# One batch's attention scores in 32 bits from TensorE transposes, in an attention and expert-layer kernel with a new instruction order

## The chip, the cores and the metric

The kernel runs on 1 core of one Trainium2 chip, as one program. The metric is the device time of one execution in microseconds (us). The engines are called PE (TensorE, matrix products), PEld (its weight loads), DVE (VectorE), ACT (ScalarE), POOL (GpSimd) and SP (SyncE, which here issues all DMAs).

## What is computed

Attention with 8 batches, 8 heads, 512 local and 32 global tokens per batch and 64 values per head. Global queries see all 544 keys; a local query sees the 32 global keys and the local keys within 32 positions. The result, 4352 tokens of 512 values, goes through a two-layer network with a piecewise-quadratic activation. All inputs and outputs are float32; the harness holds w_in and w_out as 64-bit words, which the kernel decodes itself.

```python
s_g = scale * (q_g @ k_all.T);  out_g = sm(s_g) @ v_all
s_ll = where(|pos_q - pos_k| <= 32, scale * (q_l @ k_l.T), -1e9)
s_l = concat([scale * (q_l @ k_g.T), s_ll]);  out_l = sm(s_l) @ concat([v_g, v_l])
x = concat([out_g, out_l]).transpose(0, 2, 1, 3).reshape(B * S, H * D)      # 4352 x 512
h = x @ w_in                                                                # 512 x 2048
g = where(h >= 1, h, where(h <= -1, 0, (h + 1) ** 2 / 4))
out = g @ w_out                                                             # 2048 x 512
```

## The kernel before, in words

**Precision.** Nearly all products run in float16: each operand is scaled by a power of two and split into a high and a low half, and two or three half products are summed. For queries and keys this means per batch: norms (`scale_k`, `scale_q`, lines 652 and 674), scaled splits (`nat_split`, line 707: ACT or POOL makes the high half, DVE or POOL the low half), transposes of the two halves to head-major tiles (`turn`, line 426: eight TensorE transposes into a bank and one copy out, or a DMA transpose), and for the queries a second tile with the halves swapped (`swap_q`, line 786: two SBUF-to-SBUF DMAs). `att_a` (line 858) then multiplies, for a block of 128 local queries (index i, 0 to 3) and a pair of heads (index pr, 0 to 3), the query tile and its swapped twin with each key range; there are two ranges of 128 and 64 columns for i = 0 and 3, and three of 128, 64 and 32 for i = 1 and 2. A fused DVE operation adds the mask and finds the maximum, ACT exponentiates, the probabilities are split and transposed, `att_b` (line 931) multiplies them with the values, `att_x` (line 956) divides. `glob_a` (line 1008) makes the scores of the global queries, four heads side by side in column strips of the array.

**Batch 0.** Its probabilities for i = 0 and 1 are already kept in float32 (`T["exactpv"]=2`): transposed in 32 bits on TensorE and multiplied with unsplit values. There the second product of a head has 64 rows for i = 0 and 96 rows for i = 1. A second switch, `T["exact"]`, selects 32-bit score products for the first batches; it is 0, so no batch takes that path.

**Experts.** A step s covers 256 tokens; batch b gives steps 2b and 2b+1. `win_decode` and `wout_decode` (lines 445 and 498) turn 32 blocks of 64-bit words into float32 on DVE, with ACT or POOL making parts; `win_halves` and `wout_split` make float16 halves. `moe1` (line 1138) is the first layer, four groups of 512 hidden units each for two tiles of 128 tokens; `act` the activation; `moe2` (line 1239) the second layer. From step 2 on `moe_f` does the first layer with seven instead of eight block products.

**Order.** The steps are recorded in a list by due times (`at`, line 1280), cut into segments of one engine each, and replayed in the order of a table of segment numbers (`ORDER`, line 1473); a second table (`SLOTS`) says which of 48 SBUF rooms, 6 larger ones and 8 PSUM banks each tile takes, and strings in `T` say which engine does each copy, split and cast. So one engine's instructions stand in one fixed sequence, and a waiting instruction holds back all behind it. Input loads are issued by SP with at most five on the way:

```python
if len(loads) >= AHEAD:
    tc.add_manual_dep(r.ins, loads[-AHEAD].ins.name, ...)
```

All instructions are issued from line 1461 of the file (DMA loads from 1463), so rows are told apart by the names of their tiles: `room`, `bank` and `twin` are the SBUF rooms and PSUM banks, `weights_w` the expert weights.

## Time and profile before

| | |
|---|---|
| median of 3 runs | 907.37 us (904.98 to 909.11) |
| profiled execution | 907.72 us, of it the span 906.0 us |
| mean granted TensorE clock | 0.996 of full speed |
| PE busy | 867.5 us (96%) |
| DVE busy | 750.1 us (83%) |
| ACT busy | 661.7 us (73%) |
| POOL busy | 358.3 us (40%) |
| DMA | 133.9 MB, mean 148 GB/s |

The span runs from the first to the last instruction; 1.7 us of the execution lie around it. PE is the busiest engine. The shares are means over a program whose first hundred microseconds are unlike the rest.

### The profile page before, as it was taken

Reading aid. Unit: us, or ns where it says so; the run is one execution under the profiler, and the core shown is the slowest. Engines: PE = TensorE matmul, PEld = TensorE weight load, DVE = VectorE, ACT = ScalarE, POOL = GpSimd, SP = SyncE. Lnnn points to the kernel's source line nnn. Section 1 sums busy time; section 2 is a strip of 40 time slices with the busy share of each in tenths; the row PEclk is TensorE's granted clock in tenths of the full one; section 3 lists DMA queues with packets and bytes.
Section 4 is the critical chain, followed back from the end, with each engine's and each line's share of the span. In section 5 each row is a group of like instructions: output and inputs, shape, how many; then the busy total and the mean of one; then the engine's idle time right before and its main releaser. Section 6 shows DMA issues by size and latency. Waiting matters only on the chain. (4 is left out here: it accounts for less than half of the span.)

```text
span 906.0 us, 30503 instructions
## 1 busy us (share of the span) xinstructions
PE 867.5 (96%) x12132; PEld 652.0 (72%) x12132; DVE 750.1 (83%) x2128; ACT 661.7 (73%) x1628; POOL 358.3 (40%) x406
## 2 busy tenths in 40 slices
PE   3798999999999999999999999999999999999998
PEld 2467876779686778767786866868786768687853
DVE  4989999989989897979878987887879788877651
ACT  4778998878887797688677668787868766555440
POOL 5314786444514333432343134262425432415230
PEclk9989999999999999999999999999999999999999
DMA  9989987999998999798977867968994965472101
GB/s 265 269 214 242 215 153 141 182 155 164 185 160 136 171 183 187 131 155 164 161 148 120 135 143 128 162 140 158 173 170 97 150 114 107 89 136 31 31 1 47
DMA packets 405680, 133.93 MB, mean 148 GB/s; under 512 B 382241, under 2 KB 391457, under 8 KB 405537
## 3 DMA queue, kind: packets, MB, share of 16 engines
q1 hardware_dynamic: 405536, 131.98, 79.2%
q8 instruction: 95, 1.56, 0.7%
q14 instruction: 49, 0.39, 0.2%
HBM read 44.56 MB, written 8.91 MB: 59 GB/s over the span
## 5 line engine op out<-in xcount | busy, mean ns | idle before, releaser
L1461 PEld LDWEIGHTS <-room 128*128 128x128 f16 (+2 forms) x4952 | 284.8, 98 | 203.2 <-issue 15.8
L1461 PE MATMUL bank<-weights_w,room 128*128 128x512 f16 x1632 | 370.1, 379 | 0.0
L1461 POOL TENSOR_TENSOR room<-room,room 128x512 f16<-128x512 f32 (+2 forms) x193 | 200.8, 1051 | 274.7 <-ACT room L1461 234.6
L1461 PEld LDWEIGHTS <-weights_w 128*128 128x128 f16 (+1 forms) x3968 | 221.3, 98 | 24.3 <-DVE weights_w L1461 12.9
L1461 PE MATMUL bank<-room,weights_w 128*128 128x128 f16 (+1 forms) x3840 | 225.3, 216 | 1.5 <-DVE small_nb L1461 0.8
L1461 ACT CAST room<-room 128x512 f16<-128x512 f32 (+1 forms) x213 | 121.5, 582 | 56.6 <-DVE room L1461 39.7
L1461 POOL TENSOR_TENSOR const_pb<-room,const_pb 128x448 f16<-128x448 f32 (+1 forms) x77 | 78.9, 1026 | 163.3 <-ACT const_pb L1461 78.7
L1461 PE MATMUL bank<-room,room 128*128 128x64 f16 (+6 forms) x2688 | 135.8, 200 | 4.6 <-DVE small_nb L1461 1.4
L1461 ACT ACTIVATE room<-room,small_nb 128x224 f32<-128x224 f32 (+1 forms) x256 | 118.0, 462 | 27.9 <-DVE small_nb L1461 27.1
L1461 PE MATMUL bank<-room,twin 128*128 128x128 f16 (+1 forms) x2304 | 132.1, 216 | 0.4 <-DVE room L1461 0.4
L1461 PEld LDWEIGHTS <-twin 128*128 128x128 f16 x2304 | 123.6, 98 | 2.3 <-issue 0.5
L1461 DVE CUSTOM_DVE_ANT_0 room<-bank,const_mask,batch_small_q 128x192 f32<-128x192 f32 (+1 forms) x256 | 99.6, 427 | 22.7 <-PE bank L1461 15.7
L1461 ACT ACTIVATE room<-bank,batch_small_ms 128x512 f32<-128x512 f32 (+1 forms) x112 | 83.6, 750 | 47.6 <-DVE bank L1461 20.5
L1461 DVE SCALAR_TENSOR_TENSOR bank<-bank,batch_small_ms,room 128x512 f32<-128x512 f32 (+1 forms) x112 | 80.7, 723 | 19.4 <-ACT room L1461 19.3
L1461 DVE SCALAR_TENSOR_TENSOR room<-room,batch_small_ms,bank 128x512 f32<-128x512 f32 (+1 forms) x112 | 79.3, 713 | 1.8
L1461 ACT ACTIVATE junk_junka<-room 128x512 f16<-128x512 f32 (+2 forms) x110 | 68.6, 623 | 13.0 <-DMA room<-in_q_l_dram 9.4
L1461 ACT COPY room<-bank 128x512 f32<-128x512 f32 (+3 forms) x118 | 64.5, 561 | 17.9 <-PE bank L1461 15.3
L1461 DVE TENSOR_TENSOR room<-room,room 128x512 f16<-128x512 f32 (+1 forms) x66 | 52.8, 803 | 12.9 <-ACT room L1461 12.7
L1461 DVE SCALAR_TENSOR_TENSOR room<-room,batch_small_ms,room 128x512 f32<-128x512 f32 (+1 forms) x64 | 50.4, 789 | 5.6 <-ACT room L1461 5.0
L1461 ACT CAST const_pb<-room 128x384 f16<-128x384 f32 (+1 forms) x80 | 42.2, 529 | 13.9 <-DMA room<-const_pb 13.3
L1461 DVE TENSOR_TENSOR bank<-bank,room 128x512 f32<-128x512 f32 (+1 forms) x64 | 41.8, 658 | 11.2 <-PE bank L1461 9.4
L1461 ACT ACTIVATION_READ_ACCUMULATOR room<-room,small_nb 128x1 f32 x256 | 48.4, 189 | 0.0
(179 smaller groups left out, 954.4 us busy)
## 6 DMA issues: line engine op xcount, KB each, us to landing
room<-room SPq DMA_DIRECT2D x80, 128.0 KB, 3.1
room<-in_q_l_dram SPq DMA_DIRECT2D x32, 256.0 KB, 4.1
weights_w<-in_moe_w_in_dram SPq DMA_DIRECT2D x32, 256.0 KB, 3.9
twin<-in_moe_w_out_dram SPq DMA_DIRECT2D x32, 256.0 KB, 4.6
out_dram<-room SPq DMA_DIRECT2D x32, 256.0 KB, 2.6
room<-in_k_l_dram SPq DMA_DIRECT2D x24, 256.0 KB, 4.0
room<-in_v_l_dram SPq DMA_DIRECT2D x24, 256.0 KB, 4.0
room<-const_pb SPq DMA_TRANSPOSE x119, 3.6
```

The source lines that it names most:

```text
L1461: getattr(getattr(tc.nc, engine), op)(*a, **k)
```

## The change

The first batch takes the 32-bit path (`exact=1`), and that path is rewritten. Queries and keys are loaded in the same blocks of 128 tokens as for the other batches. `heads` (which replaces `pairs`) transposes two heads at a time in 32 bits on TensorE, four transposes per block of tokens, 40 in all; one copy takes a block of keys out of the bank, two copies a block of queries (each to a tile whose other 64 rows POOL has set to zero, so that a product over 128 rows counts one head of the pair). `scale_k`, `scale_q`, `nat_split`, `turn` and `swap_q` are not run for batch 0. `att_a` makes one 32-bit product per head and key range, 80 in all, in place of 160 in float16; `glob_a` makes 40 in place of 80. The 32-bit products of probabilities with values now have 96 rows for i = 0 too: POOL sets 32 rows of the transposed tile to zero, and `att_b` takes 96 rows of both operands. `ORDER`, `SLOTS` and the engine strings of `T` are replaced as a whole, so every engine's sequence differs throughout the program.

```diff
-    def load_pairs(src_l, src_g, b, nm, part):
-    ...
     def load(b, nm, part):
-        if EXACT(b) and nm != "v":
-            r = load_pairs(*{"k": (k_l, k_g), "q": (q_l, q_g)}[nm], b, nm, part)
-            ...
         r = load_q(b, part) if nm == "q" else load_kv(...)
-    def pairs(b, nm, c):
+    def heads(b, nm, c):
         st, n = BT[b]["raw" + nm][c]
         one = full_id()
-        ...
+        t = ps_t.tile([P, NI, n], F32, tag="p", name=f"pt{nm}{b}_{c}")
+        for hp in range(NI):
+            nc.tensor.transpose(t[:, hp], st[:n, 2 * hp:2 * hp + 2, :].rearrange("p h d -> p (h d)"), one[:n, :n])
+        return t
     def prep_k(b, c):
         if EXACT(b):
+            t = heads(b, "k", c)
+            k = (ktp if c < NI else kt4p).tile(list(t.shape), F32, ...)
+            evict(of("turns", b, c, 30, "a"), k, t)
     def prep_q(b, c):
             for u, pl in enumerate((qap, qbp)):
+                q = pl.tile([P, NI, P], F32, tag="qa" if u == 0 else "qb", name=f"q{'ab'[u]}{b}_{c}")
                 nc.gpsimd.memset(q[(1 - u) * D:(2 - u) * D], 0.0)
+                evict(who if who != "d" else "av"[u], q[u * D:u * D + D], t[u * D:u * D + D])
     def att_a(b, i, pr):
+            h = pr if EXACT(b) else 2 * pr + u
             for lo, hi, kk in regs:
-                nc.tensor.matmul(s[:, u, lo:hi], qa, kk, start=True, stop=False)
-                nc.tensor.matmul(s[:, u, lo:hi], qb, kk, start=False, stop=True)
+                if EXACT(b):
+                    nc.tensor.matmul(s[:, u, lo:hi], d["q" + "ab"[u], i][:, h], kk, start=True, stop=True)
+                    continue
+                nc.tensor.matmul(s[:, u, lo:hi], d["qa", i][:, h], kk, start=True, stop=False)
+                nc.tensor.matmul(s[:, u, lo:hi], d["qb", i][:, h], kk, start=False, stop=True)
             one, n2 = full_id(), w - P
+            if n2 < CH2:
+                nc.gpsimd.memset(pt[n2:CH2, :, 1], 0.0)
     def att_b(b, i, pr):
             if EXACT_PV(b, i):
-                n2 = WID[i] - P
     def glob_a(b, g):
+                for j in range(4) if EXACT(b) else ():
+                    h = 4 * g + j
+                    nc.tensor.matmul(s[32 * j:32 * j + 32, o:o + n], d["qa", NI][:, h // 2, h % 2], d["kt", c][:, h // 2, 0:n],
+                                     start=True, stop=True, tile_position=(0, 32 * j))
+                for qn in () if EXACT(b) else ("qa", "qb"):
-ORDER = ("2 0 3 29 31 28 35 30 34 27 13 12 67 68 69 70 89 88 90 91 92 71 93 96 10 5 4 22 6 7 8 9 111 72 73 74 94 75 97 23 24 "
...
-T = dict(exact=0, exactpv=2, es="nnnn", gramq="aaaaaaaa", dg="vvvvvvaaaaavvav", sid="vvvvv", fast=2, grams="ppaaaaaa",
+T = dict(exact=1, exactpv=2, es="vnnn", gramq="aaaaaaaa", dg="vvvaavaavaaaaav", sid="vvvvv", fast=2, grams="ppaaaaaa",
...
```

DVE's sequence at the program's start, before (`small_amk` and `small_dg` belong to the key norm of batch 0, `batch_small_q` and `batch_small_sk` to its query and key scales, `weights_w_0_66` is the first block of w_in):

```order
L1461 TENSOR_REDUCE small_amk_104<-bank_105 128x1
L1461 TENSOR_SCALAR small_amk_104<-small_amk_104 128x1 x2
L1461 TENSOR_SCALAR batch_small_q_0_116<-batch_small_q_0_116 128x2 x3
L1461 TENSOR_SCALAR small_dg_106<-const_negid_84,small_amk_104 128x128
L1461 RECIPROCAL batch_small_q_0_116<-batch_small_q_0_116 128x2
L1461 TENSOR_REDUCE small_amk_104<-bank_107 128x1
L1461 TENSOR_SCALAR batch_small_sk_108<-small_amk_104 128x1
L1461 TENSOR_SCALAR batch_small_q_0_116<-batch_small_q_0_116,batch_small_sk_108 128x2
L1461 RECIPROCAL batch_small_sk_108<-batch_small_sk_108 128x1
L1461 SCALAR_TENSOR_TENSOR room_118<-room_86,batch_small_q_0_116,room_118 128x8x64
L1461 TENSOR_SCALAR weights_w_0_66<-weights_w_0_66 128x512
L1461 SCALAR_TENSOR_TENSOR bank_91<-bank_91,weights_w_0_66 128x512
```

and the same place in the change:

```order
L1424 MEMSET const_c_0_111 128x1 x2
L1424 COPY room_115<-bank_102 128x512
L1424 TENSOR_SCALAR weights_w_0_66<-weights_w_0_66 128x512
L1424 SCALAR_TENSOR_TENSOR bank_91<-bank_91,weights_w_0_66 128x512
L1424 TENSOR_SCALAR room_99<-weights_w_0_67 128x512
L1424 SCALAR_TENSOR_TENSOR weights_w_0_66<-weights_w_0_66,bank_91 128x512
L1424 ISA room_146,small_nb_145<-bank_132,const_mask_0_58,const_c_0_111 128x192
L1424 ISA small_nb_145 128x1
```

The norm and scale rows and the first query split are gone; one copy of a transposed block of keys stands ahead of the first decode, and the first score operations (ISA, the fused mask and maximum) stand right behind it.

SP's sequence at the start, before (loads of keys, then two blocks of queries, then the first w_in blocks):

```order
L1463 DMA room_94<-in_k_l_dram 128x8x64
L1463 DMA room_96<-in_k_l_dram 128x8x64
L1463 DMA room_93<-in_k_l_dram 96x8x64
L1463 DMA room_97<-in_k_g_dram 32x8x64
L1463 DMA room_95<-in_k_l_dram 128x8x64
L1463 DMA room_97<-in_k_l_dram 32x8x64
L1463 DMA room_93<-in_k_g_dram 32x8x64
L1463 DMA room_87<-in_q_l_dram 128x8x64
L1463 DMA room_86<-in_q_l_dram 128x8x64
L1463 DMA weights_w_0_69<-in_moe_w_in_dram 128x2x256
L1463 DMA weights_w_0_66<-in_moe_w_in_dram 128x2x256 x2
```

and in the change:

```order
L1426 DMA room_86<-in_q_l_dram 128x8x64
L1426 DMA weights_w_0_68<-in_moe_w_in_dram 128x2x256
L1426 DMA room_93<-in_k_g_dram 32x8x64
L1426 DMA room_94<-in_k_l_dram 128x8x64
L1426 DMA room_93<-in_k_l_dram 96x8x64
L1426 DMA weights_w_0_66<-in_moe_w_in_dram 128x2x256
L1426 DMA weights_w_0_70<-in_moe_w_in_dram 128x2x256
L1426 DMA weights_w_0_66<-in_moe_w_in_dram 128x2x256
```

The second half of the first w_in block, which the first decode needs, moves from the twelfth load to the eighth; three of the five key blocks move behind it.

TensorE's first score products of batch 0, before (`room_119` and `room_121` are the query tile and its swapped twin, `room_115` and `room_123` two key tiles; one head pair):

```order
L1461 MATMUL bank_105<-room_115,room_119 128x128
L1461 LDWEIGHTS room_121
L1461 MATMUL bank_105<-room_115,room_121 128x128
L1461 LDWEIGHTS room_119
L1461 MATMUL bank_105<-room_123,room_119 128x64
L1461 LDWEIGHTS room_121
L1461 MATMUL bank_105<-room_123,room_121 128x64
```

and in the change (`room_113` and `room_114` are the two query tiles, `room_112` and `room_115` the key tiles; one head pair):

```order
L1424 MATMUL bank_102<-room_110,room_94 128x128 x4
L1424 MATMUL bank_100<-room_110,room_93 128x128 x4
L1424 MATMUL bank_132<-room_112,room_113 128x128
L1424 MATMUL bank_132<-room_115,room_113 128x64
L1424 MATMUL bank_132<-room_112,room_114 128x128
L1424 MATMUL bank_132<-room_115,room_114 128x64
```

The 32-bit products need no separate weight-load instruction in the program, and the first of them stand directly behind the transposes of the first key blocks, ahead of the first w_in norms.

## Rows read from the trace of the kernel before

**Rows 1.** Busy time by stretch of the span: stretch in us, its length, then busy us and count for PE, PEld, DVE, ACT and POOL, the granted TensorE clock, the DMA share and GB/s.

```profile
0.00:14.50 14.50, 2.66 (x21) 2.07 (x21) 2.69 (x14) 3.96 (x7) 7.80 (x23) 1.00 1.01 218
14.50:80.00 65.50, 52.36 (x418) 37.76 (x419) 60.12 (x185) 53.67 (x125) 24.18 (x31) 0.95 0.99 255
80.00:112.60 32.60, 29.23 (x503) 27.59 (x501) 32.35 (x100) 29.61 (x66) 22.05 (x23) 1.00 1.10 223
112.60:800.00 687.40, 681.52 (x9893) 513.20 (x9891) 594.83 (x1719) 532.89 (x1351) 276.44 (x301) 1.00 0.85 149
800.00:906.00 106.00, 101.71 (x1309) 71.41 (x1306) 60.11 (x114) 41.56 (x81) 27.78 (x30) 1.00 0.23 44
```

**Rows 2.** What PE waited for from 0 to 112.6 us: total us, times, longest.

```profile
PE bank L1461 <- DVE weights_w L1461: 12.3, 7, 5.4
PE bank L1461 <- DMA room<-in_k_g_dram: 9.1, 1, 9.1
PE bank L1461 <- DVE room L1461: 2.8, 3, 1.6
PE bank L1461 <- DVE small_dg L1461: 1.4, 1, 1.4
```

**Rows 3.** Timeline of PE, merged, around the first product of the first expert layer and around the first of the second layer: start, us, what.

```profile
80.13 2.84 PE L1461 MATMUL bank<-room,weights_w 128*128 128x128 f16 x48
...
112.59 2.75 PE L1461 MATMUL bank<-weights_w,room 128*128 128x512 f16 x12
```

**Rows 4.** Timeline of DVE from 8 us on: start, us, what, and in brackets the idle time before it with what ended it.

```profile
11.49 0.29 DVE L1461 TENSOR_REDUCE small_amk<-bank 128x1 f32<-128x128 f32 x1 [10.43 <-PE bank L1461]
...
13.87 0.73 DVE L1461 SCALAR_TENSOR_TENSOR room<-room,batch_small_q,room 128x512 f16<-128x512 f32 x1
14.52 0.42 DVE L1461 TENSOR_SCALAR weights_w<-weights_w 128x512 int32<-128x512 int32 x1
15.05 0.70 DVE L1461 SCALAR_TENSOR_TENSOR bank<-bank,weights_w 128x512 int32<-128x512 int32 x1
```

**Rows 5.** Timeline of SP's DMA issues from 6 to 15 us: start, us, what. The two query loads are the eighth and ninth load, the weight loads begin with the tenth.

```profile
6.63 1.01 SPq L1463 DMA_DIRECT2D room<-in_q_l_dram  x2
8.38 6.93 SPq L1463 DMA_DIRECT2D weights_w<-in_moe_w_in_dram  x10
```

**Rows 6.** DMA issues from 8 to 16 us: what, count, size, median us from issue to landing.

```profile
weights_w<-in_moe_w_in_dram SPq DMA_DIRECT2D x11, 256.0 KB, 3.8
```

**Rows 7.** Groups of DVE instructions from 0 to 112.6 us, shapes apart: what, count, busy us, mean ns of one, idle before.

```profile
L1461 DVE SCALAR_TENSOR_TENSOR room<-room,batch_small_q,room 128x512 f16<-128x512 f32 x3 | 2.2, 740 | 0.0
L1461 DVE SCALAR_TENSOR_TENSOR room<-room,batch_small_sk,room 128x512 f16<-128x512 f32 x2 | 1.9, 936 | 0.3 <-ACT room L1461 0.3
L1461 DVE SCALAR_TENSOR_TENSOR room<-room,batch_small_sk,room 64x512 f16<-64x512 f32 x1 | 0.7, 735 | 0.0
L1461 DVE SCALAR_TENSOR_TENSOR room<-room,batch_small_q,room 32x512 f16<-32x512 f32 x1 | 0.7, 734 | 0.0
L1461 DVE TENSOR_SCALAR batch_small_q<-batch_small_q 128x3 f32<-128x3 f32 x3 | 0.6, 193 | 0.0
L1461 DVE TENSOR_SCALAR room<-room,batch_small_sk 128x512 f16<-128x512 f32 x1 | 0.5, 481 | 0.0
L1461 DVE TENSOR_SCALAR room<-room,batch_small_q 128x512 f16<-128x512 f32 x1 | 0.5, 478 | 0.0
L1461 DVE CAST weights_w<-bank 128x512 f16<-128x512 f32 x1 | 0.7, 660 | 0.0
```

**Rows 8.** Timeline of PE from 53.8 to 54.7 us and from 89 to 94.3 us, in 32 bits and in float16. A 32-bit product shows as two matmul records, a transpose as one.

```profile
53.94 0.61 PE L1461 MATMUL bank<-room,room 128*128 128x128 f32 x4
54.47 0.40 PE L1461 MATMUL bank<-const_ident,room 64*128 64x64 f16 x8
...
90.30 1.06 PE L1461 MATMUL bank<-room,room 128*128 128x64 f32 x8
91.19 2.85 PE L1461 MATMUL bank<-room,weights_w 128*128 128x128 f16 x48
93.88 0.28 PE L1461 MATMUL bank<-room,room 128*128 128x128 f16 x2
93.99 0.22 PE L1461 MATMUL bank<-kt_kt,room 128*128 128x64 f16 x2
94.05 0.28 PE L1461 MATMUL bank<-room,room 128*128 128x128 f16 x2
94.16 0.22 PE L1461 MATMUL bank<-kt_kt,room 128*128 128x64 f16 x2
94.22 0.28 PE L1461 MATMUL bank<-room,weights_w 128*128 128x128 f16 x2
```

**Rows 9.** Groups of PE instructions over the whole span, shapes apart, columns as in rows 7. The transposes through `const_ident` are those of batch 0; half of the bf16 products of `room` with itself are the key norm of batch 0; `qg_qga` are the global queries of all batches.

```profile
L1461 PE MATMUL bank<-room,qg_qga 128*32 128x128 f16 x256 | 9.2, 222 | 0.0
L1461 PE MATMUL bank<-const_ident,room 128*128 128x128 f16 x64 | 6.7, 274 | 2.3 <-DVE room L1461 2.3
L1461 PE MATMUL bank<-room,room 64*128 64x64 f32 x16 | 4.0, 333 | 0.0
L1461 PE MATMUL bank<-room,room 96*128 96x64 f32 x16 | 3.1, 275 | 0.0
L1461 PE MATMUL bank<-room 128*128 128x128 bf16 x32 | 2.9, 262 | 9.1 <-DMA room<-in_k_g_dram 9.1
```

**Rows 10.** Busy time by stretch from 55 to 72 us, columns as in rows 1.

```profile
55.00:60.00 5.00, 3.96 (x29) 2.36 (x27) 4.61 (x23) 3.00 (x9) 2.39 (x3) 1.00 0.84 217
60.00:61.00 1.00, 1.00 (x6) 0.81 (x5) 1.00 (x3) 1.00 (x3) 0.00 (x0) 0.66 0.83 205
61.00:66.00 5.00, 5.00 (x28) 3.34 (x29) 5.00 (x22) 2.49 (x6) 0.00 (x0) 0.50 0.54 149
66.00:67.00 1.00, 1.00 (x7) 0.98 (x5) 1.00 (x6) 1.00 (x2) 0.31 (x1) 0.50 0.42 92
67.00:72.00 5.00, 5.00 (x36) 3.49 (x35) 4.24 (x8) 4.52 (x15) 2.21 (x3) 0.99 0.91 234
```

**Rows 11.** Groups of POOL instructions from 0 to 14.5 us, columns as in rows 7.

```profile
L1461 POOL MEMSET const_pb<- 128x1024 f16 x2 | 1.8, 952 | 0.0
```

75 lines of the change are left out of this document (13 added, 62 removed), and 492 rows, old and new, of tables (ORDER, SLOTS).

## The prediction

> **What bounds the kernel now.** I read the busy time by stretch first. From 112.6 to 800 us PE works 681.5 of 687.4 us, and in the tail 101.7 of 106 [rows 1]: there PE is the bound, and time is won or lost only by PE's own work. The first 112.6 us are different. From 14.5 to 112.6 us (98.1 us) DVE works 60.12 + 32.35 = 92.5 us, PE 52.36 + 29.23 = 81.6, ACT 53.67 + 29.61 = 83.3 and POOL 46.2 [rows 1]: DVE is the fullest engine and PE has 16.5 us to spare. The waits of PE say the same: 12.3 us went to tiles of w_in that DVE was still decoding, 2.8 to other DVE results, 9.1 (one wait, at the start) to the load of the last keys [rows 2]. The timeline of PE gives the two milestones that count: the first expert product at 80.13 us and the first of the second layer at 112.59 [rows 3]. What moves the second one earlier moves the end earlier, provided PE does not get more to do behind it.
>
> The start, 0 to 14.5 us, is a chain of its own. DVE does nothing of weight until 11.49 us, when the key norm's sums arrive from PE; it then works through norm and scale rows and one query split, and only at 14.52 begins the first w_in decode [rows 4]. The loads agree: the query blocks are the eighth and ninth issue, at 6.63 us, the weights follow from 8.38 [rows 5], and a weight block lands 3.8 us after its issue [rows 6].
>
> So I cut the run into A (0 to 14.5), B (14.5 to 112.6, DVE's) and C (behind it, PE's). The profiled execution took 907.72 us with a span of 906.0; the median of the runs is 907.37, a third of a microsecond less, which I neglect. About 0.5% (4.5 us) is what a measurement of this kernel can tell from no change: faster means below 902.8, slower above 911.9.
>
> **A, the start.** Removed from DVE: the norm, scale and split rows between 11.49 and 14.52, 3.0 us in all [rows 4]. Added: one copy of a transposed key block, like the 128x512 cast out of a bank, 0.66 us [rows 7]. The second half of the first w_in block moves from the twelfth load to the eighth. The eighth was issued at 6.63 [rows 5]; with 3.8 us to land [rows 6] that is 10.4. The copy stands ahead of the decode on DVE and waits for load, transpose and bank, so I put the decode at 11.0: **-3.5 us**. Bounds: 0 (the three key blocks now behind the weights, or the copy's own wait, give it back) and -4.1 (decode right at landing). POOL gets more at this place: eight zeroings of 64 rows by 512 float32, 2 KB per partition, which is the size of the memset that took 0.952 us [rows 11], 7.6 us in all. POOL is busy 7.80 of 14.5 us in A and 24.18 of 65.5 behind it [rows 1], so they fit beside other work and I cost them at nothing. Without that cover, that is, if a mask that the first score operation needs queues behind them on POOL, they cost 4 (the half that the first two query blocks need) to 7.6 us.
>
> **B, DVE's work.** The splits of batch 0's keys and queries go: 2.2 + 1.9 + 0.7 + 0.7 + 0.5 + 0.5 = 6.5 us [rows 7], of which the one at 13.87 (0.73) was counted in A, so 5.8. Of some 20 small norm and scale operations, 0.19 us each [rows 7], about seven lie in B: 1.4. Together **-7.2**, say -7. The stretch holds 5.6 us of DVE idle time. Bounds: 0, if the casts and subtractions that the new engine strings hand to DVE (18 more in the whole program, at about 0.66 each 12 us; most lie behind B) fall in B, and -12.8, if the idle time goes with the work. ACT loses the high halves as well, so it is not the next bound; SP loses ten query-swap DMAs, and nothing waits for those any more.
>
> **B, PE's work.** One 32-bit product replaces two half products. In the timeline four 32-bit products of 64 columns go from 90.30 to 91.19, 0.222 us each; eight half products that make two heads' scores go from 93.88 to 94.22, 0.34 us; four 32-bit transposes of 128 columns go from 53.94 to 54.47, 0.13 each [rows 8]. Scores: 80 x 0.222 = 17.8 us, where the 160 half products took 160/8 x 0.34 = 6.8 at most: +11. No row shows a 32-bit product of 128 columns; if its cost doubled with the columns, 32 of them would take 7.1 more, if it went with the transposes' 0.13 the 80 would take only 10.4. I stay with 0.222, since the operation is the same. Transposes: 40 x 0.13 = 5.2 for 80 x 6.7/64 = 8.4 [rows 9]: -3.2. Key norm: half of 2.9 [rows 9] and its like for the queries, -2. The 96-row products: 3.1 us for 16 where 64 rows take 4.0 [rows 9], -0.4 for eight. Net +5 to +6 in B, up to +12.5 at the dear end. PE has 16.5 us to spare there, so at first it hides beside DVE's work. It does not hide where DVE itself waits for a product: a mask operation that waits for a pair of heads now waits for 0.9 us of PE instead of 0.34. I take **+1** for that, between 0 (all covered) and 2 x 5.6 = 11 (DVE's present idle time tripled).
>
> The Trainium skill ("FP8 and Floating Point Precision", section "TensorE Precision Notes") says that a true FP32 product is four passes through the array. By columns the 80 products have 32 x 128 + 32 x 64 + 16 x 32 = 6656, four times over at 2.4 GHz 11.1 us (an estimate from that page), against 17.8 by the row. The row speaks against a price by passes alone: 64 columns took 0.222 us where four passes are 0.107. By the page the sum would be some 0.5 us lower, since few of these products lie behind B.
>
> **C, behind 112.6 us.** Of the 80 score products 72 stand before the first second-layer product on PE, so eight are left, 8 x 0.222 - 8 x 0.085 = +1. The 40 products of the global queries all lie behind it. Nearest row: the float16 ones of that shape, 9.2/256 = 0.036 each [rows 9], 80 of them 2.9 us. In 32 bits one costs between 0.072 (two records of that row, as rows 8 shows two per product) and 0.222: 2.9 to 8.9, so 0 to +6. I take +1, nearer to the lower end, since four of them stand side by side in column strips like those of that row. Sum of C **+2**, bounds 1 and 7. Whatever else the new order does to the 687 us is not in the diff, and I put it at 0.
>
> **Sum.** 907.7 - 3.5 - 7 + 1 + 2 = 900.2: **900 us**, 0.8% faster. With the ends: 907.7 - 4.1 - 12.8 + 0 + 1 = 892, and 907.7 + 0 + 0 + 7 = 915. The dear end of DVE's waiting (+11) would come on top only if it fell together with those, which is the second rival's case.
>
> **Rivals.**
> *PE, or the weights' arrival, takes DVE's place in B.* PE would have 81.6 + 6 = 88 of 98 - 7 = 91 us, and the DMA engines are already at 0.99 and 1.10 in that stretch [rows 1]. Then a DVE that is done sooner waits for products or blocks, and B gives only some 4 of its 7, with A's 3.5 given half back: about 904 (900 to 908). For: PE's and the loads' fill. Against: the swap DMAs go, and PE's longest waits were for DVE. Chance 0.20.
>
> *The products come into DVE's chain (slower).* The new order puts the first scores of batch 0 on DVE directly behind the first decode. If key blocks, which now load behind weights, and 0.9 us of products per pair hold DVE there, the decodes queued behind are late, and PE's 12.3 us of waiting for them [rows 2] grow. A gives nothing, B loses 2 although its work shrank (DVE idle up from 5.6 to about 15), C takes +6: 916. The point that decides: the first expert product after 80.1 us. Chance 0.17.
>
> *It does more than it says: the order.* ORDER and SLOTS are new as a whole. C has 5.9 us of PE idle time and the tail 4.3 [rows 1]; if the new order adds 6 to these 10, the gain shrinks to 906. It would show as new waits of PE behind 112.6 us while both milestones come earlier as forecast. Chance 0.11.
>
> *The clock.* From 61 to 67 us PE ran at a granted clock of 0.50, which is 1.2 GHz; in the five microseconds before, it was busy 3.96 us with 29 matmuls, and it stood at full rate again from 67 [rows 10]. Six microseconds at half rate cost about 3.2. With the 32-bit products elsewhere the low stretch can go (-3.2, 897) or come three times as long (+6.4, 907). I give the long one 0.05. [...]
>
> **How the numbers follow.** Forecast 0.47, then 0.20, 0.17, 0.11 and 0.05. Faster: nearly all of the forecast and a bit of the first rival, 0.50. Slower: the second rival, with a little from the third, 0.18. The rest, 0.32, is no change. The likeliest case by itself spans 894 to 905. The range 892 to 914 takes in the first, third and fourth rivals and half of the second.
>
> **What would show it.** Right: the first decode on DVE near 11 us; the first expert product near 72 us and the first second-layer product near 102 to 103; DVE idle in B at about 6 us or less; 32-bit score products 0.22 us apart; PE busy behind the first second-layer product up by 1 to 7 us. Wrong: the first expert product at 80 or later (second rival); milestones that come earlier but an end that does not (third); PE waiting in B for loads instead of for w_in tiles from DVE (first); a granted clock of 0.5 over more than 6 us (fourth).

## The result, and the profile after

The changed kernel took **913.35 us** (median of 6 runs, 911.09 to 914.22), the kernel before 906.56 beside it (6 runs, 904.98 to 909.11): ratio 1.0063, 95% interval 1.0046 to 1.0080. It is slower, by 6.8 us between the medians and 5.7 by the ratio, where 7.7 less had been forecast. The profiled execution took 913.89 us with a span of 912.1; before it was 907.72 with 906.0, so the two profiles stand 6.1 us apart.

The busy time by stretch of the kernel after, columns and cuts as in [rows 1], with one cut more at 140 us:

```profile
0.00:14.50 14.50, 7.99 (x36) 6.88 (x36) 5.33 (x8) 4.65 (x7) 12.61 (x35) 1.00 0.93 260
14.50:80.00 65.50, 58.43 (x422) 46.75 (x421) 57.66 (x187) 51.65 (x128) 22.99 (x28) 0.87 0.94 242
80.00:112.60 32.60, 29.84 (x468) 26.67 (x468) 29.37 (x82) 26.42 (x65) 18.69 (x20) 1.00 1.05 208
112.60:140.00 27.40, 22.12 (x254) 15.44 (x252) 25.07 (x73) 20.54 (x51) 15.84 (x18) 0.81 0.82 145
```

Three things differ from [rows 1]: POOL is busy 12.61 us of A instead of 7.80, the granted clock is 0.87 in the first part of B instead of 0.95, and behind 112.6 us, where I had PE as the bound, PE is idle for 5.3 of 27.4 us. (Before, that last stretch had PE busy for all of its 27.40 us.)

PE's timeline after, at the two milestones of [rows 3] and at a third one, the first product of the next step's first layer (the rows of the third show only what lies inside the view, 17 and 13 of 48 products):

```profile
72.89 2.84 PE L1424 MATMUL bank<-room,weights_w 128*128 128x128 f16 x48 [0.16 <-ACT weights_w L1424]
...
104.94 2.75 PE L1424 MATMUL bank<-weights_w,room 128*128 128x512 f16 x12
...
135.06 1.11 PE L1424 MATMUL bank<-room,weights_w 128*128 128x128 f16 x17
```

The same third product in the kernel before:

```profile
127.29 0.89 PE L1461 MATMUL bank<-room,weights_w 128*128 128x128 f16 x13
```

Both milestones that I had named came earlier, by 7.24 and 7.65 us. The third came 7.77 **later**. From there to the end the two kernels take nearly the same time: 778.7 us before, 777.0 after. So nearly everything is decided between the first instruction and the third milestone, and the lead is lost between the second and the third.

Cut at these milestones instead of at fixed times, the kernel before (columns as in [rows 1]):

```profile
0.00:80.13 80.13, 55.15 (x442) 39.96 (x442) 62.94 (x198) 57.76 (x132) 31.98 (x53) 0.96 0.99 249
80.13:112.59 32.46, 29.09 (x501) 27.45 (x498) 32.21 (x100) 29.47 (x66) 22.04 (x23) 1.00 1.10 222
112.59:127.29 14.70, 14.70 (x199) 8.81 (x196) 14.55 (x52) 14.59 (x42) 13.23 (x15) 1.00 1.01 157
127.29:906.00 778.71, 768.54 (x11000) 575.81 (x10998) 640.39 (x1782) 559.87 (x1392) 291.00 (x316) 1.00 0.77 134
```

and the kernel after:

```profile
0.00:72.89 72.89, 59.65 (x367) 47.18 (x368) 56.27 (x176) 49.73 (x120) 30.73 (x59) 0.88 0.93 245
72.89:104.94 32.05, 31.28 (x503) 29.63 (x503) 30.63 (x89) 27.34 (x65) 21.62 (x23) 1.00 1.05 224
104.94:135.06 30.12, 22.51 (x214) 13.99 (x212) 26.59 (x76) 22.61 (x58) 14.26 (x16) 0.83 0.88 151
135.06:912.10 777.04, 768.30 (x10992) 574.92 (x10990) 640.68 (x1779) 548.73 (x1361) 294.04 (x317) 1.00 0.75 133
```

This is the reading that I lacked. Behind the third milestone PE and DVE work the same time in both (768.5 and 768.3, 640.4 and 640.7; ACT works 11 us less after). Up to it DVE works 62.94 + 32.21 + 14.55 = 109.7 us before and 56.27 + 30.63 + 26.59 = 113.5 after: not 7 less but 3.8 more. The new order gives DVE less ahead of the first product and 12 us more between the second and the third milestone. The early milestones were bought with postponed work. DVE's idle time up to the third milestone is 127.29 - 109.7 = 17.6 before and 135.06 - 113.5 = 21.6 after, and 3.8 + 4.0 is the whole 7.8. That is so by definition, since the time up to a milestone is an engine's work and its idle time; what caused them is asked below. The same sum for PE gives 98.9 us of work before and 113.4 after, with less idle time; whether that growth counts, e3 and e15 test.

A milestone on PE need not divide DVE's queue at the same instruction. Here 3.4 us of key splits of batch 1 lie ahead of the third milestone after, and behind it before (batch 0 has none after; one row of each, after and before):

```profile
124.58 1.43 DVE L1424 SCALAR_TENSOR_TENSOR room<-room,batch_small_sk,room 128x512 f16<-128x512 f32 x1
...
133.66 2.37 DVE L1461 SCALAR_TENSOR_TENSOR room<-room,batch_small_sk,room 128x512 f16<-128x512 f32 x2
```

**The 3.8 us of work.** DVE's timeline after, from its first bank copy on, idle time before each in brackets:

```profile
7.96 0.69 DVE L1424 COPY room<-bank 128x512 f32<-128x512 f32 x1 [6.89 <-PE bank L1424]
9.94 3.32 DVE L1424 TENSOR_SCALAR weights_w<-weights_w 128x512 int32<-128x512 int32 x1 [1.28 <-DMA weights_w<-in_moe_w_in_dram]
```

The decode starts at 9.94, even before the 11.0 that I had put. But this instruction took 0.42 us before [rows 4] and takes 3.32 here. POOL's timeline after at that place:

```profile
9.49 1.84 POOL L1424 MEMSET const_pb<- 128x1024 f16 x2
11.28 1.16 POOL L1424 MEMSET const_pgb<- 128x1280 f16 x1
...
12.42 0.52 POOL L1424 MEMSET room<- 64x512 f32 x1
```

and before, the same zeroings:

```profile
3.81 1.84 POOL L1461 MEMSET const_pb<- 128x1024 f16 x2
5.59 1.16 POOL L1461 MEMSET const_pgb<- 128x1280 f16 x1
```

Before, they ran while DVE had nothing to do. The zeroings of the query tiles now stand ahead of them on POOL (nine from 1.94 to 6.53 us, 0.5 us each; with a tenth at 12.42 they are ten, not the eight of the forecast), and the old ones fall on the first decode, which ends at 13.26, just behind them.

The other 0.9 is a balance: the splits and norm rows of batch 0 gone, against what the new engine strings hand to DVE and the splits of batch 1 that stand earlier. DVE's groups up to the eighth activation of the first step (0 to 124.7 us after), columns as in [rows 7]:

```profile
L1424 DVE TENSOR_SCALAR weights_w<-weights_w 128x512 int32<-128x512 int32 x9 | 6.7, 744 | 1.3 <-DMA weights_w<-in_moe_w_in_dram 1.3
...
L1424 DVE CAST weights_w<-bank 128x512 f16<-128x512 f32 x3 | 2.0, 680 | 4.2 <-PE bank L1424 4.2
...
L1424 DVE TENSOR_TENSOR room<-room,room 128x512 f16<-128x512 f32 x2 | 1.4, 685 | 0.5 <-ACT room L1424 0.5
...
L1424 DVE TENSOR_SCALAR room<-weights_w,const_wo 128x512 f32<-128x512 f32 x2 | 1.0, 483 | 0.0
...
L1424 DVE CAST const_pb<-room 128x448 f16<-128x448 f32 x1 | 0.8, 812 | 0.0
```

The splits of batch 0 are gone as said, but three casts stand where [rows 7] has one, and the subtractions, scalings and the cast below them are new on DVE here, some 4 us together. The first row, 4.5 us before, holds the first decode.

**The 4.0 us of idle time.** PE's clock after, three low stretches (columns as in [rows 1]):

```profile
18.00:34.00 16.00, 12.25 (x66) 10.27 (x64) 14.89 (x47) 8.29 (x19) 2.95 (x5) 0.50 1.05 318
...
114.00:120.00 6.00, 4.50 (x31) 2.99 (x24) 5.49 (x15) 4.51 (x13) 3.52 (x4) 0.50 0.70 69
...
126.00:130.00 4.00, 3.53 (x21) 1.60 (x21) 3.90 (x11) 2.03 (x5) 3.29 (x4) 0.60 1.03 220
```

The clock is at its low level, 1.2 GHz, for some 25 us, where [rows 10] shows 6. The granted clock alone does not tell it all: in the trace of e5 (below) it reads 1.00 from 18 to 34 us, and yet the twelve 32-bit products from 28.59 us take 5.35 us, as in the kernel after; in e13, which fills PE's waits ahead of them, they take 2.86. After, and then e13:

```profile
28.61 5.36 PE L1424 MATMUL bank<-room,room 128*128 128x128 f32 x24
...
28.61 2.86 PE L1430 MATMUL bank<-room,room 128*128 128x128 f32 x24
```
What PE waited for from 105 to 140 us after (total, times, longest); before, no wait is listed there:

```profile
PE bank L1424 <- ACT small_dg L1424: 3.8, 1, 3.8
PE bank L1424 <- DVE weights_w L1424: 2.3, 2, 1.9
PE bank L1424 <- DVE small_nb L1424: 1.5, 1, 1.5
```

The longest is for the diagonal of the third w_out norm, which the new strings give to ACT; there it stands behind a row of exponentials (at 126.02 us).

The prices of the new products, PE's timeline after at full rate, two records to a product:

```profile
78.64 0.44 PE L1424 MATMUL bank<-room,room 128*128 128x128 f32 x2
78.91 0.33 PE L1424 MATMUL bank<-kt_kt,room 128*128 128x64 f32 x2
...
121.56 1.08 PE L1424 MATMUL bank<-room,room 128*32 128x128 f32 x32
122.45 0.24 PE L1424 MATMUL bank<-kt_kt,room 128*32 128x32 f32 x8
```

From 78.64 to 78.91 a 32-bit product of 128 columns costs 0.27 us; one of 64 columns costs 0.17 (the next one starts at 79.08), 0.22 in the mean; a global one costs 0.89/16 = 0.056.

### The profile page after: what moved, and what is told of

The parts are those of the page before. It is cut to its first block, busy times and chain, and to the rows that moved or that the text cites. A ratio compares the mean times of both kernels' runs of the same rounds, so it can differ in the third digit from the quotient of the medians.

```text
span 912.1 us, 30350 instructions
## 1 busy us (share of the span) xinstructions
PE 881.7 (97%) x12070; PEld 665.7 (73%) x12070; DVE 754.2 (83%) x2118; ACT 648.4 (71%) x1601; POOL 360.6 (40%) x413
## 5 line engine op out<-in xcount | busy, mean ns | idle before, releaser
L1424 PEld LDWEIGHTS <-room 128*128 128x128 f16 (+2 forms) x4692 | 269.3, 98 | 191.8 <-issue 9.3
L1424 POOL TENSOR_TENSOR room<-room,room 128x512 f16<-128x512 f32 (+3 forms) x195 | 204.1, 1058 | 236.5 <-ACT room L1424 214.6
L1424 PE MATMUL bank<-room,room 128*128 128x64 f16 (+7 forms) x2792 | 158.9, 210 | 10.0 <-DMA room<-in_q_l_dram 4.2
L1424 POOL TENSOR_TENSOR const_pb<-room,const_pb 128x448 f16<-128x448 f32 (+1 forms) x72 | 74.7, 1039 | 176.6 <-ACT const_pb L1424 74.8
L1424 ACT ACTIVATE room<-room,small_nb 128x192 f32<-128x192 f32 (+1 forms) x256 | 118.1, 462 | 22.5 <-DVE small_nb L1424 21.8
L1424 DVE CUSTOM_DVE_ANT_0 room<-bank,const_mask,batch_small_q 128x192 f32<-128x192 f32 (+1 forms) x224 | 87.1, 427 | 21.8 <-PE bank L1424 17.2
L1424 ACT COPY room<-bank 128x512 f32<-128x512 f32 (+5 forms) x123 | 63.6, 529 | 42.6 <-PE bank L1424 32.0
L1424 ACT ACTIVATE junk_junka<-room 128x512 f16<-128x512 f32 (+2 forms) x105 | 65.5, 624 | 5.5 <-DMA room<-in_v_l_dram 2.2
L1424 DVE TENSOR_TENSOR room<-room,room 128x512 f16<-128x512 f32 (+1 forms) x63 | 47.9, 763 | 8.8 <-ACT room L1424 8.7
L1424 PEld LDWEIGHTS bank<-room,room 128*128 128x128 f32 (+3 forms) x344 | 41.0, 192 | 13.8 <-issue 7.9
```

The costliest lines, as they stand in the source:

```text
L1424: getattr(getattr(tc.nc, engine), op)(*a, **k)
```

## Experiments

Ratios are to the kernel before on the same chip. The changed kernel was not run again on each of these chips, so what a run gains or loses against it is a difference of two ratios, given below in us of 906.6, and known to some 2 us either way (3 for e4). Four theories were open: PE's new 32-bit work, DVE's work, the order behind the second milestone, and (from the trace after) the zeroings and the clock. A table of all runs stands at the end of this section.

**PE's work and DVE's work, in both kernels.** The kernel before with the score products of the first batch issued three times:

```
-            for lo, hi, kk in regs:
+            for lo, hi, kk in regs * (3 if b == 0 else 1):
```

> The kernel before, each of batch 0's 160 half-precision score products issued three times (same result): 320 more at 0.0425 us = +13.6 us of PE work in the old order, nothing on DVE, no wait added. Theory W (PE's own work before the expert products is on the path, also where PE shows idle time, because products and DVE's work follow each other in a chain): +9 to +13 us, about 917. Theory Q (such work hides beside DVE's, as the forecast had it, and the changed kernel lost its time in the order of PE's queue behind the first second-layer product): +1 to +3 us, about 908.5.

It took 913.19 us, ratio 1.0074 [1.0054, 1.0094]: 13.6 us more PE work (an estimate; PE's busy time grew by 9.4) cost 6.7 at the end, between the two theories. PE's "16.5 us to spare" cover half of it.

The kernel before without the low halves of that batch's keys and queries (zeros in their place, 5 us less on DVE):

```
-        nc.vector.scalar_tensor_tensor(lo, src, s[:np_, 0:1], hi, op0=ALU.mult, op1=ALU.subtract)
+        getattr(nc.vector, low)(lo, src, s[:np_, 0:1], hi, op0=ALU.mult, op1=ALU.subtract)
...
+                    if op == "no_low":          # low="no_low" for the first batch
+                        tc.nc.vector.memset(a[0], 0.0)
```

> The kernel before, the low halves of batch 0's queries and keys set to zero by a short DVE memset instead of the fused split (their share of the scores is left out): DVE loses 6.5 us of splits and gets some 1.5 us of memsets, -5 us in the first 112.6 us; PE's work is the same. The forecast's term for B (DVE's work is the bound): -4 to -5 us, about 902. Theory W: 0 to -2 us, about 906, since PE's work is on the path as well.

904.39 us, 0.9979 [0.9967, 0.9992]: 5 us off the fullest engine gave 1.9 (0.7 to 3.0). The third milestone did not move (127.38 us, DVE working 4.9 us less and idling 5.0 more up to it); in this profile the gain lies behind it, 776.6 us instead of 778.7.

The kernel after with the local score products taken from the upper 16 bits of keys and queries, so in one bf16 product each:

```
-                    nc.tensor.matmul(s[:, u, lo:hi], d["q" + "ab"[u], i][:, h], kk, start=True, stop=True)
+                    qh, kh = [x.bitcast(BF16).rearrange("p (c t) -> p c t", t=2)[:, :, 1] for x in (...)]
+                    nc.tensor.matmul(s[:, u, lo:hi], qh, kh, start=True, stop=True)
```

> The changed kernel, with batch 0's 80 local score products taken from the upper 16 bits of both operands (the rest of the words is left out), so one pass instead of a 32-bit product; order, tiles and DVE's work as in the change. PE loses 80 x (0.222 - about 0.06) = 13 us. Theory W: -8 to -12 us against the changed kernel's 913.4, about 903. Theory Q: 0 to -3, about 912, with the waits of PE between 105 and 131 us as long as before or longer.

911.85 us, 1.0063 [1.0043, 1.0083]: 13 us less PE work by the estimate, 9.6 by PE's busy time up to the third milestone (103.9 instead of 113.4), and nothing gained by the ratio, 1.5 us by the medians; the third milestone came 0.6 us earlier. The 32-bit products are not what the change lost. PE's longest wait from 105 to 140 us in that run is the one of the kernel after:

```profile
PE bank L1425 <- ACT small_dg L1425: 4.0, 1, 4.0
```

The kernel after with the mask operations of the first batch done twice (10.9 us more on DVE):

```
-        for u in range(2):
+        for u in (0, 1, 0, 1) if b == 0 else (0, 1):
```

> The changed kernel, with batch 0's 32 fused mask operations done twice on DVE (same result): 32 x 0.34 = +10.9 us of DVE work between 15 and 121 us. If DVE still sets the pace there: +8 to +11 us, about 923. If PE's work does (theory W): +0 to +4, about 915. Theory Q has no number of its own here: DVE's delay shows in full only behind 105 us, +3 to +6.

919.62 us, 1.0153 [1.0124, 1.0182]: 8.2 us on top by the ratios, 6.3 by the medians, so 0.6 to 0.75 for each us added to DVE.

**The order.** Segments of the order moved in the kernel after, by their numbers: ACT's diagonal ahead of the exponentials (e5), PE's postponed rows earlier (e6), both (e7).

```
     order = [int(x) for x in ORDER.split()]
+    for n, ahead_of in [(710, 463)]:                                             # e5
+    for n, ahead_of in [(702, 711), (757, 711), (721, 775), (642, 775), (626, 706)]:   # e6
+        order.remove(n)
+        order.insert(order.index(ahead_of), n)
```

> The changed kernel with one instruction moved in ACT's queue: the diagonal of the third w_out norm (small_dg, at 126.02 us) goes ahead of a cast, the two exponentials of the global scores and a split, to where its input is ready (about 122.3). Theory Q (the waits of PE between 105 and 131 us come from single rows that stand too late or too early in a queue): PE's longest wait there, 3.8 us, goes, and with it some half-clock time; -3 to -5 us against the changed kernel's 913.4, about 909. Theory D (DVE and ACT have that much work left at this place, and PE would only wait at the next row): 0 to -1, about 913.

> The changed kernel with five pieces of PE's queue moved, nothing added or left out: the products of one global block go ahead of the last w_out norm's, two score products and the second output products ahead of the key norm of batch 1, and 24 products of the fourth attention block and the second hidden group ahead of the third w_out norm's diagonal. So PE has work where it waited 1.9, 1.5 and 3.8 us. Theory Q: those 7.2 us and part of the half-clock time go, -5 to -9 us, about 906. Theory D: the rows that were moved ahead aren't ready either or the norms come later for it; 0 to -2, about 912.5.

> Both moves together, the ACT row and the five pieces of PE's queue. Theory Q: the larger of the two gains and a little more, -6 to -10 us against the changed kernel, about 905. Theory D: 0 to -3, about 911.5.

912.00, 911.25 and 911.58 us (1.0039, 1.0047, 1.0039): one and a half to two us each, hardly clear of the noise, and together no more. With the wait for ACT gone, PE waited for the next late things, from 105 to 140 us in e7:

```profile
PE bank L1427 <- DVE room L1427: 3.6, 2, 2.3
PE bank L1427 <- ACT gpf_gpf L1427: 1.9, 1, 1.9
PE bank L1427 <- DVE small_nb L1427: 1.2, 1, 1.2
```

That is how 12 us of postponed DVE work would look from PE: whichever wait is removed, the next result of DVE or ACT is late.

**The zeroings.** The three zeroings of const_pb and const_pgb given to DVE, at the head of its queue:

```
-        nc.gpsimd.memset(t, 0.0)
+        nc.gpsimd.zero_on_dve(t, 0.0)     # replayed as nc.vector.memset; const_pgb likewise
```

> The changed kernel, with the three large zeroings that POOL does from 9.49 to 12.4 us (const_pb twice, const_pgb) done by DVE instead, first in its queue, where it waits anyway until 7.96 us. In the changed kernel the first decode on DVE (a 128x512 int32 operation that took 0.42 us before) lasts 3.32 us, from 9.94 to 13.26, as long as POOL's zeroings run. Theory Z (POOL's zeroings hold it up): it takes about 0.4 us, the decodes come 2 to 2.9 us earlier, and the end 1 to 2 us earlier than the changed kernel's, about 911.5. Rival (its length has another cause, the second half of the block still landing): it still lasts about 3 us; 0.

909.02 us, 1.0021 [1.0004, 1.0038], against the 1.0063 of the change: 3.8 us of the loss (1.6 to 6.0), more than the 1 to 2 expected. DVE's timeline in that run:

```profile
0.98 1.03 DVE L1424 MEMSET const_pb<- 128x512 uint32 x2 [0.98 <-PEq L1722]
...
9.59 0.79 DVE L1427 TENSOR_SCALAR weights_w<-weights_w 128x512 int32<-128x512 int32 x1 [1.28 <-DMA weights_w<-in_moe_w_in_dram]
```

DVE does the zeroings in 1.6 us while it has nothing else, and the first decode takes 0.79 instead of 3.32, beside one zeroing of a query tile that POOL still does there (9.53 us, 0.52 long).

**The clock.** Products of ones with ones, overwritten by the norm product behind them, at places where PE waits: late (e8: 20 and 64 of them between 112 and 126 us) and early (e13: 16 ahead of the first w_in norm, 10 and 8 ahead of two transposes, 16 each ahead of two norm products, at 27 and 49 us; so 50 of the 66 lie where the expectation puts them all):

```
         t = ps_s.tile([P, P], F32, tag="p", name=f"am{name}")
+        for _ in range({"k1": 20, "wo2": 64}.get(name, 0)):      # e8; e13: {"w": 16}
+            nc.tensor.matmul(t, ones, ones, start=True, stop=True)
...
+            for _ in range(0 if f else 16):                       # e13, ahead of the first w_in norm
+                nc.tensor.matmul(W["n"], ones, ones, start=True, stop=True)
...
+        for _ in range({"k2": 10, "q1": 8}.get(f"{nm}{c}", 0)):   # e13, ahead of transposes
+            nc.tensor.matmul(t[:, 0], ones, ones, start=True, stop=True)
```

> The changed kernel with 20 and 64 idle products (ones times ones, into the bank that the next product starts anew) ahead of the two norm products at 115.99 and 126.47 us, for which PE waits 1.5 and 3.8 us. They fill the waits with work that counts for nothing. If the granted clock of 0.50 around 114 to 120 and 126 to 130 us is a cost of its own, it stays at 1.00 there and the end comes 2 to 4 us earlier, about 910.5; if what the products wait for is late anyway and the clock only slows work that waits, 0 to +1, about 913.5.

> The changed kernel with 66 idle products of 128 columns (ones times ones, into banks that the next product starts anew) at four places of PE's queue where it waits between 14.7 and 28.5 us (ahead of the first w_in norm product, of two blocks of transposes, and of the norm's diagonals). In the changed kernel the granted clock is 0.50 from about 18 to 34 us; the twelve 32-bit score products from 28.61 take 5.4 us, and DVE then waits 4.2 us (35.4 to 39.6) for products that stand behind them. If the clock is a cost of its own there: it stays or comes back to 1.00 before 28 us, that wait falls to 2 us or less, and the end comes 1 to 2 us earlier, about 912. If the loads of w_in (DMA share 1.0 until about 38 us) set the pace of that stretch: the wait moves, the end doesn't, 0 to +0.5.

911.42 us, 1.0043 [1.0027, 1.0059], and 909.66 us, 1.0034 [1.0013, 1.0055]: some 1.8 and 2.6 us back, the first within the noise and the second just outside it. The low stretches are gone where they were filled, in e8

```profile
114.00:120.00 6.00, 5.70 (x82) 4.17 (x80) 5.45 (x24) 4.22 (x12) 2.29 (x3) 1.00 0.84 177
126.00:130.00 4.00, 4.00 (x30) 2.47 (x29) 3.90 (x13) 2.53 (x5) 2.77 (x3) 1.00 1.13 185
```

and in e13

```profile
18.00:34.00 16.00, 14.70 (x112) 12.00 (x111) 14.89 (x47) 9.62 (x22) 2.89 (x5) 1.00 1.05 311
```

The same in the kernel before, 12 and 12 idle products ahead of its low stretch of [rows 10]:

```
+        for _ in range({'v0': 12}.get(name, 0)):
+            nc.tensor.matmul(t, ones, ones, start=True, stop=True)
...
+            for _ in range(12 if W["f"] == 8 else 0):
+                nc.tensor.matmul(o[:, 0:P], ones, ones, start=True, stop=True)
```

> The kernel before with 24 idle products of 128 columns (ones times ones) at the two places between 55.7 and 57.9 us where PE waits half a microsecond each (ahead of a w_in product and of the value norm's diagonal). There the granted clock fell to 0.50 from about 60.5 to 66.9 us. If the clock is a cost of its own in this order too: it stays at 1.00 and the end comes 1 to 3 us earlier, about 905. If what follows waits for DVE anyway (theory D in the old order): 0 to +0.5.

909.31 us, 1.0012 [0.9995, 1.0030]: nothing gained, 0.5 us at the most. The low stretch did not go as expected but became half as long (some 3.4 us at half rate instead of 6.7, worth some 1.7 us of PE's work; columns as in [rows 1]):

```profile
61.00:66.00 5.00, 5.00 (x32) 3.55 (x32) 5.00 (x23) 2.83 (x7) 0.00 (x0) 0.66 0.89 221
```

DVE is busy for all of these 5 us with the idle products or without [rows 10], which is why PE's rate should cost little there; half of the stretch was not tested. Where another engine waits for PE it shows: DVE's one wait of 4.2 us for a w_in bank at about 35 us is 1.3 in e13.

**Put together.** Zeroings and both sets of idle products (e14); zeroings and half words (e15); e14 with ACT's row of e5 (e17).

> The changed kernel with POOL's three zeroings done by DVE and the idle products at both places (14.7 to 28.5 us, and the 84 ahead of the norm products at 116 and 126 us). If the gains add (3.8 for the zeroings, 1.8 for the late products, 0 to 2 for the early ones): 906 to 908, level with the kernel before. If they are one gain: 909.

> The changed kernel with DVE's zeroings, and the 80 local score products from the upper 16 bits alone (the rest of the words is left out): 13 us less PE work, with the hold-up of the first decode gone. If PE's 32-bit work costs little in this order also without the hold-up: 907.5 to 909. If it was hidden behind the hold-up and is now on the path: 4 to 8 us less than with the zeroings alone, about 903.

> The changed kernel with DVE's zeroings, the idle products at both places and ACT's one row (the third w_out norm's diagonal) moved ahead to where its input is ready. The version before it was level with the kernel before; the row alone gave 2 us in the changed kernel and idle products fill the same wait of PE. If they are the same gain: 907 to 908. If the row's earlier place counts on its own: about 905.5.

907.51 us, 0.9994 [0.9979, 1.0009]; 909.06, 1.0012 [0.9995, 1.0029]; 907.61, 1.0004 [0.9987, 1.0022]. With the zeroings moved and the clock largely kept up (in e14 still 0.79 from 18 to 34 us), the loss is gone, and nothing is won: 6.3 us back against the change, 2.4 of them (0.4 to 4.5) against the zeroings alone. e15 takes 11 us of PE's busy time away and gains 0.8 us against the zeroings alone, within the noise. e14, cut at its three milestones:

```profile
0.00:71.05 71.05, 61.59 (x432) 50.34 (x433) 56.27 (x179) 50.11 (x120) 27.44 (x56) 0.95 0.93 255
71.05:103.37 32.32, 31.40 (x503) 29.68 (x503) 30.55 (x90) 27.46 (x66) 21.59 (x23) 1.00 0.97 216
103.37:128.78 25.41, 22.97 (x299) 16.57 (x297) 24.02 (x73) 20.84 (x54) 14.31 (x16) 1.00 0.76 165
```

DVE's work up to the third milestone is 56.27 + 30.55 + 24.02 = 110.8 us, 1.1 more than the 109.7 of the kernel before (the 110.8 hold 1.6 for the zeroings), and its idle time 128.78 - 110.8 = 17.9 against 17.6: nearly the same work up to the milestone, the same idle time, the same end. Behind it DVE works 643.3 us instead of 640.4, so part of its work has only slid behind the milestone, where PE is the bound.

**Three that gained nothing more.** The moves of e5 and e6 and one more, with the zeroings (e10); letters of the strings changed so that eight casts, subtractions and halves leave DVE, 5.4 us in all (e11); everything without idle products (e12).

```
-  casts="aavaaaaavaa..."  halves="aahaahhaabac..."      # e11; subs[10], subs[15], glow[3], glow[5]: v to p
+  casts="aavaaaaaaaa..."  halves="aaaaaaaaabac..."
```

> The changed kernel with DVE's zeroings as in the run before it, the moved ACT row and the five moved pieces of PE's queue, and one more piece of PE's queue moved: the second output products of the first 128 tokens (ready since about 108 us) go from behind the w_in combination at 132 us to ahead of the second global block at 121 us. If PE's waits from 105 to 131 us are a matter of where rows stand as far as other work is ready: 2 to 3 us more than the moves alone, about 908. Theory D (what DVE and ACT still have to do sets when the next step can begin): the first product of step 1 moves by no more than the decodes did, about 910.

> The changed kernel with eight instructions of the first 125 us put back from DVE to ACT or POOL by the engine strings: three casts of w_in low halves (0.67 us each) and one cast of probabilities (0.8) to ACT, two subtractions of probabilities and two of the activation's halves (0.65 each) to POOL; -5.4 us of DVE's work, none added or left out. Theory D (DVE's work up to the last activation of step 0 sets the pace, and the new strings gave back what the missing splits saved): -3 to -4 us against the changed kernel's, about 910. Rival (the order alone): 0 to -1, or slower, since ACT and POOL get the work at fixed places of their queues.

> The changed kernel with all of it: DVE's zeroings, the moved rows of ACT and PE, and the eight instructions taken off DVE. If the gains add: about 906, level with the kernel before; if they are one gain seen three ways: about 909.

909.19 us, 1.0028 [1.0011, 1.0046]; 914.59, 1.0088 [1.0063, 1.0113]; 913.05, 1.0061 [1.0042, 1.0080]. In e10 the third milestone stood at 127.19, as before, and the end was no earlier than in e9, because PE's next instructions were late (PE's timeline):

```profile
127.19 2.84 PE L1430 MATMUL bank<-room,weights_w 128*128 128x128 f16 x48
132.63 0.53 PE L1430 MATMUL bank<-room,room 128*128 128x64 f16 x12 [2.59 <-DVE room L1430]
```

In e11, with some 5 us less to do (749.4 us in the whole run instead of 754.2), DVE stood still for 7.1 us:

```profile
44.30 0.70 DVE L1424 SCALAR_TENSOR_TENSOR bank<-room,weights_w 128x512 int32<-128x512 int32 x1 [7.10 <-issue]
```

The shift that this decode needs stands on ACT behind the casts that I had given to ACT, and these wait for PE; the decode starts 1.3 us later than in the kernel after (43.04 us). An engine is relieved only if its work doesn't land ahead of what it waits for.

The kernel before had medians of 906.16 to 907.95 us beside these runs, so they are compared by the ratio. Medians in us, and milestones of the profiled execution: first expert product, first second-layer product, first product of the next step.

| run | median | ratio | first | second | third |
|---|---|---|---|---|---|
| before | 906.56 | 1 | 80.13 | 112.59 | 127.29 |
| after | 913.35 | 1.0063 | 72.89 | 104.94 | 135.06 |
| e1 before, products x3 | 913.19 | 1.0074 | 85.20 | 116.08 | 133.12 |
| e2 before, no low halves | 904.39 | 0.9979 | 79.07 | 112.71 | 127.38 |
| e3 half words | 911.85 | 1.0063 | 76.17 | 106.52 | 134.44 |
| e4 masks twice | 919.62 | 1.0153 | 79.03 | 112.96 | 140.81 |
| e5, e6, e7 order | 912.00, 911.25, 911.58 | 1.0039, 1.0047, 1.0039 | 74.52, 73.27, 74.89 | 105.65, 104.43, 106.09 | 132.75, 132.61, 133.57 |
| e8 fill late | 911.42 | 1.0043 | 74.48 | 105.63 | 130.96 |
| e9 zeroings | 909.02 | 1.0021 | 71.94 | 103.06 | 130.69 |
| e10, e11, e12 | 909.19, 914.59, 913.05 | 1.0028, 1.0088, 1.0061 | 71.78, 76.58, 73.63 | 104.03, 107.74, 104.83 | 127.19, 135.71, 129.51 |
| e13 fill early | 909.66 | 1.0034 | 70.25 | 102.30 | 129.89 |
| e14 zeroings and fills | 907.51 | 0.9994 | 71.05 | 103.37 | 128.78 |
| e15 zeroings, half words | 909.06 | 1.0012 | 70.90 | 102.75 | 129.78 |
| e16 before, fill | 909.31 | 1.0012 | 79.67 | 113.37 | 128.04 |
| e17 e14 and ACT's row | 907.61 | 1.0004 | 69.73 | 100.33 | 125.59 |

No version beats the kernel before by more than the measurement can tell, save e2, which leaves part of the computation out. A single profile's third milestone says little to a us or two: e17's lies 1.7 us before that of the kernel before, and its median doesn't.

## Why the prediction was wrong

The forecast was 7.7 us faster, and it became 6.8 slower (5.7 by the ratio). By its own steps:

- **A, the decode's start: right; its cover: wrong.** "They fit beside other work and I cost them at nothing." I asked whether a mask on POOL would queue behind the new zeroings (it didn't matter, and each took 0.5 us, not 0.95, ten of them instead of eight). I did not ask where the *old* zeroings would go, nor who would then run beside them: 2.9 us on DVE's first decode, some 3.8 at the end (e9). The Trainium skill ("SBUF — State Buffer", section "SBUF: two separate sides") has GpSimd and certain VectorE instructions share one pair of ports, which one instruction holds alone while the other stands still. The trace agrees: 0.42 became 3.32, and the copy out of a bank at 7.96 kept its 0.69 beside POOL's mask work. That it was this pair no run here isolates.
- **B, DVE's work: the step that failed most.** "Together -7.2", with the returning casts as a bound of 0, since "most lie behind B". Some 4 us of such rows lie ahead of the third milestone, and the new order drew 3.4 us of splits of batch 1 there as well: DVE's work up to the third milestone grew by 0.9 us without the hold-up, and over the whole run from 750.1 to 754.2. DVE's idle time in B became 11.1 us, where 6 or less was the sign of being right. And had the work shrunk by 7, e2 says that the end would have moved by some 0.4 of it, 2.7 us: I took a us on the fullest engine for a us at the end.
- **The milestone: wrong.** "What moves the second one earlier moves the end earlier, provided PE does not get more to do behind it." Behind it PE got 7.6 us more work by the trace, part of it the low clock, and 7.6 us of waiting; DVE got 12 us more between that milestone and the next. I had read PE's density behind 112.6 us in the trace before, and took it over to an order that was new.
- **B, PE's work: price right, cover wrong in principle.** 0.222 forecast, 0.22 measured. But PE's spare time hides only half of such work there (e1: 0.5 of each us in the old order); in the new order, taking 13 us away gave nothing that can be told from none (e3, e15).
- **C: the work right, the place wrong.** The global products cost 0.056, even below the lower end of 0.072. From the second milestone to the end PE works 768.30 + 22.51 = 790.8 us instead of 768.54 + 14.70 = 783.2, a little over my upper bound of 7, and part of that is the low clock: two groups of twelve products take 3.85 and 4.36 us where 2.75 is the full rate. What I left out were 7.6 us of waiting.

Of the rivals, **the order** had the signature right (both milestones earlier, new waits of PE behind them), but with 6 us for what came to 7.6 of waits and more work besides. **The clock**, given 0.05, came about four times as long as before by the granted clock, in stretches where I had not looked; idle products against it gave some 2.4 us back on top of the zeroings (e14 against e9). The Trainium skill ("TensorE: Matmul & The Clock Gate", section "HAM oscillation") lets pauses between bursts bring the low rate; the trace agrees in so far as the low stretches stand where PE waited (it was busy 1.11 us of the 3.5 ahead of the one at 18 us, and 2.70 of the 6 ahead of the one at 126), and products put into those waits kept the rate up. The second rival's point of decision was not reached: the first product came at 72.89. That PE or the loads took DVE's place is not shown; the DMA engines are near full in B in both kernels, and no run changed the loads.

Shown, then: the zeroings cost some 3.8 us and the low clock some 2.4 more, together 6.3 (4.2 to 8.3, e14), which is the loss within the noise. One by one the two sets of idle products gave 1.8 and 2.6; with the zeroings that would be 8.2, so the gains do not simply add. Shown by the cut at milestones: DVE's work did not shrink as forecast. Not shown is that a smaller sum would have won the time: in e2 the third milestone stood still with 5 us less. So why nothing is won beyond the loss stays partly open. Not settled either is what sets DVE's 17 to 18 us of idle time up to the third milestone, the same before and in e14, though the first decode starts 4 us earlier there (10.20): in e14 DVE waits for PE and for loads in the start, and no run took one of these away alone.

## What to carry to other kernels

Cut the trace at the milestone behind which the two kernels do the same work, and sum each engine's work up to it: a milestone that comes earlier proves nothing if the order has put the work behind it. When work is added to an idle engine's queue, follow what it pushes back and which instruction of another engine will then run beside that. Where several engines are nearly full, measure the slope (add or remove a known amount) before taking a us on one of them for a us at the end; here it was 0.4 to 0.75, and next to nothing for PE work taken away in the new order. Check too what has crossed the milestone: an engine's queue is not divided at the same instruction in two orders.

## What the runs showed of the hardware

- POOL's zeroings stretch a 128x512 int32 operation of DVE from SBUF to SBUF from 0.42 to 3.32 us; with three of them moved it takes 0.79 (e9) and 0.43 (e14).
- Idle products keep the granted clock at 1.00 where it was 0.50 or 0.60 (e8, e13; in e14 the early ones only reach 0.79), at no cost that shows, since PE was waiting there.
- A granted clock of 1.00 in the trace does not by itself mean the full rate: from 18 to 34 us it reads 0.50 in the kernel after and 1.00 in e5, and the same twelve products take 5.36 and 5.35 us.
- A 32-bit product of 128 columns costs 0.27 us, one of 64 columns 0.17, one in a 32-column strip 0.056.
